# A new written order for the first two batches of a fused attention and expert-layer kernel

## The chip, the cores and the metric

The kernel runs on one core of one Trainium2 chip. The metric is the device time of one execution, in microseconds. Three runs of the kernel before took 465.88, 466.14 and 466.8 us; the median is 466.14 us. TensorE is called PE below, VectorE DVE, ScalarE ACT, GpSimd POOL and SyncE SP, as in the profile.

## What is computed

```python
def sm_attn(qq, kk, vv):
    s = scale * np.matmul(qq, kk.transpose(0, 1, 3, 2))
    a = np.exp(s - np.max(s, axis=-1, keepdims=True))
    a = a / (np.sum(a, axis=-1, keepdims=True) + 1e-09)
    return np.matmul(a, vv)
p_packed = sm_attn(p, k, v)             # 32 packed rows attend to 576 keys
out = sm_attn(q, p_packed, p_packed)    # 576 queries attend to the 32 packed rows
...
h = np.maximum(np.maximum(x @ w1, x @ w2), x @ w3)
return h @ w_out
```

There are 8 batches of 8 heads with 576 positions and a head size of 64. x is `out` with the heads of a position side by side (4608 x 512); w1, w2 and w3 are 512 x 768 and w_out is 768 x 512. All of it is float32.

## The kernel before

The kernel works batch by batch. The matrix x is never formed: `p_packed @ w` is made first (P, `project`, L439), and the second attention's weights are then multiplied with it. To keep float32 accuracy, both sides of the large products are cut into a high and a low part, and three matmuls take the place of one.

The stages of a batch, with the letters that the written order gives them:

- k, v, q, w: loads, all issued on SP's queue (L159, L165, L166, L174, L153). k of a batch comes in two transfers of 640 KB with p beside it, q in two of 576 KB, v in two of 512 KB with a small one of 64 KB each. A w chunk is 512 KB; there are 24 of them. `w02` is chunk 2 of column block 0 of w1, w2 and w3; `w60` to `w65` are w_out.
- C (`convert`): a chunk arrives as pairs of 32-bit words and is made into float32 in four steps: two on ACT (L188, L193), one on DVE (L202), one on POOL (L206). W (`weights`) prepares w_out.
- S (`scores`, L253), A (`weigh`, L266 to L271): first attention's scores, their row maximum on DVE and the exponential on ACT. The weights are then turned: in the first two batches by PE (`turn`, L296, L297) with copies out of PSUM, from the third batch on by X (`spread`): two transposes on DVE (L313) and sixteen small transfers on SP's queue (L319).
- V (`values`, L337), K (`packed`, L352): the product with v, and its turned form `pt`.
- Q (`queries`, L366), B (`attend`): second attention; nine steps on DVE, POOL and ACT for each half of the heads.
- P (`project`): `p_packed @ w` on PE, then the high part on ACT (L450) and the low part on DVE (L452).
- N (`layer_in`, L475): the main product, 36 groups of six matmuls per batch, each group into one PSUM bank. `N01` takes the next group of batch 0 and column block 1, and so on. E (`maximum`, L489, and a copy of L129 or L131): the maximum over w1, w2 and w3, which frees those banks. There are four such banks for N and for the output product together.
- H (`operands`, `halves`, L513, L134): operands of the output product. O (`layer_out`, L544): 14 groups of nine matmuls per batch. F (`finish`, L560 to L592): scaling, sums and stores.

Two tables of words, `START` and `LOOP`, set the order of everything. `run` takes the words one after another; each word takes one step of its stage's generator, so that the order of the words is the order of the instructions on each engine and on SP's queue. A last letter `v`, `g` or `a` puts the step on DVE, POOL or ACT, where the stage allows a choice:

```python
for at, word in enumerate(words.split()):
    name = word.rstrip("vga")
    chosen[0] = word[len(name):] or None
    ...
    if kind in loads:
        loads[kind](*x)
    else:
        if key not in begun:
            begun[key] = stages[kind](*x)
        next(begun[key], None)
```

`START` holds batches 0 and 1 whole, the first part of batch 2 (its first attention, its queries and some of `B20`, `B21`, `P20` to `P22`), all weights, and the k loads of batch 3. `LOOP` is run six times and holds the rest of a batch beside the beginning of the next. Words `J` and `I` with a number put that many 128-column matmuls of the identity on PE (`rouse`, L143): `J` at once, `I` ahead of the next stage that has a place for them. They compute nothing.

Buffers come from pools with a fixed number of slots: eight for k, q, v, the turned weights and the maxima ("b"), six for w chunks and w_out ("xs"). A load waits on SP's queue until the last reader of its slot is done, and all loads behind it on that queue wait too.

## Time and profile before

| What | Value |
|---|---|
| median of three runs | 466.14 us (465.88 to 466.8) |
| span of the profiled execution | 464.4 us |
| what lies around the span, against the median | 1.7 us |
| PE busy | 455.2 us (98%) |
| DVE busy | 333.5 us (72%) |
| POOL busy | 247.9 us (53%) |
| ACT busy | 159.9 us (34%) |
| granted PE clock | 1.00 |
| part set by `START` | from the beginning to the scores of batch 3, which PE starts at 141.74 us |

A profile page gives busy time by engine, the span in 40 slices of 11.6 us, and the chain of work that ended last. A busy PE also counts the identity matmuls. Matmuls of N stand in the trace as `mi` (L475), those of the output product as `mo` (L544), of P as `pw` (L439), scores of either attention as `s` (L253, L366), the product with v as `pa`, `tp` or `av` (L337).

### The profile page before, as it was taken

What the parts mean: (1) busy time and instruction counts of PE and PEld (TensorE: products, weight loads), DVE (VectorE), ACT (ScalarE), POOL (GpSimd) and SP (SyncE); (2) the same over time, 40 slices, a digit from 0 to 9 for tenths busy, and PEclk for the clock granted to TensorE, in tenths of its full rate; (3) what the DMA queues carried; (4) which work ended last, traced back from release to release, by engine and by line L of the source; (5) the groups of instructions that cost most, each with busy time, mean ns of one, the idle gap of its engine ahead of it and who ended that gap; (6) DMA issues with size and microseconds to landing.
All of it is one profiled execution on the core that took longest, in us unless ns stands there. A gap on an engine that the chain in (4) does not pass through costs nothing.

```text
span 464.4 us, 11561 instructions
## 1 busy us (share of the span) xinstructions
PE 455.2 (98%) x4724; PEld 404.9 (87%) x4724; DVE 333.5 (72%) x698; ACT 159.9 (34%) x341; POOL 247.9 (53%) x213
## 2 busy tenths in 40 slices
PE   7999998999999999999999999999999999999996
PEld 3477887899899898998899988998989988998996
DVE  1799987888887678566887479766786668845552
ACT  2787856535322126022331025121260223302130
POOL 0468875574542675526572384706764275725832
PEclk9999999999999999999999999999999999999999
DMA  8999846010316430256004450065202540020002
GB/s 313 398 382 355 321 98 230 1 58 25 95 66 195 135 119 1 80 160 233 2 27 152 87 211 2 27 199 155 94 1 94 151 116 1 28 76 1 2 6 97
DMA packets 35780, 55.66 MB, mean 120 GB/s; under 512 B 17296, under 2 KB 26512, under 8 KB 35728
## 3 DMA queue, kind: packets, MB, share of 16 engines
q1 hardware_dynamic: 35728, 54.93, 35.4%
q8 instruction: 37, 0.61, 0.5%
q14 instruction: 15, 0.12, 0.1%
HBM read 41.94 MB, written 9.44 MB: 111 GB/s over the span
## 4 chain that ended last, share of the span: by engine, by line
PE 88%; DMA 5%; SPq 3%; DVE 3%; issue 1%; ACT 1%; DVEq 0%
PE mi L475 44%; PE mo L544 29%; PE pw L439 6%; PE idle L143 2%; SPq L319 2%; PE s L366 2%; PE av L337 2%; DMA wi<-in_wi 2%; PE s L253 2%; DMA q<-in_qt 1%; DMA kt<-in_kp 1%; PE tp L296 0%; DMA xt<-x 0%; SPq L159 0%; PE pa L337 0%
## 5 line engine op out<-in xcount | busy, mean ns | idle before, releaser
L475 PE MATMUL mi<-a2h,ph 128*128 128x288 f32 x576 | 173.5, 301 | 0.8 <-DVE pl L452 0.6
L475 PE MATMUL mi<-a2l,ph 128*128 128x288 f32 x576 | 169.9, 295 | 0.0
L475 PE MATMUL mi<-a2h,pl 128*128 128x288 f32 x576 | 169.6, 295 | 0.0
L489 DVE TENSOR_TENSOR r<-mi,r 128x288 f32<-128x288 f32 x192 | 84.4, 452 | 57.8 <-PE mi L475 55.3
L475 PEld LDWEIGHTS mi<-a2h,ph 128*128 128x128 f32 x576 | 108.0, 188 | 13.4 <-issue 7.0
L475 PEld LDWEIGHTS mi<-a2l,ph 128*128 128x128 f32 x576 | 108.0, 188 | 0.2
L475 PEld LDWEIGHTS mi<-a2h,pl 128*128 128x128 f32 x576 | 108.1, 188 | 0.0
L513 POOL TENSOR_TENSOR r<-r 128x288 f32<-128x288 f32 (+1 forms) x47 | 50.4, 1083 | 81.3 <-DVE r L489 65.5
L129 ACT COPY r<-mi 128x288 f32<-128x288 f32 x73 | 29.0, 399 | 185.8 <-PE mi L475 185.7
L450 ACT ACTIVATE ph<-pw 128x384 fp32r<-128x384 f32 (+1 forms) x67 | 40.2, 631 | 46.5 <-PE pw L439 43.5
L452 DVE SCALAR_TENSOR_TENSOR pl<-pw,ph 128x384 fp32r<-128x384 f32 (+1 forms) x67 | 46.2, 713 | 9.5 <-ACT ph L450 9.2
L544 PE MATMUL mo<-ych,xl 128*128 128x288 f32 x144 | 42.5, 295 | 0.0
L544 PE MATMUL mo<-ych,xh 128*128 128x288 f32 x144 | 42.4, 294 | 0.0
L544 PE MATMUL mo<-ycl,xh 128*128 128x288 f32 x144 | 42.3, 294 | 0.0
L439 PE MATMUL pw<-w_sb,pt 64*32 64x384 f32 x768 | 36.3, 487 | 0.1
L206 POOL TENSOR_TENSOR w_sb<-w_sb,wi 128x512 int32<-128x512 int32 x18 | 23.9, 1336 | 22.0 <-DVE w_sb L202 17.4
L134 POOL TENSOR_TENSOR ybl<-r,ybh 128x576 fp32r<-128x576 f32 x15 | 21.7, 1448 | 19.7 <-DVE ybh L131 16.2
L134 POOL TENSOR_TENSOR ycl<-r,ych 128x864 fp32r<-128x864 f32 x12 | 26.6, 2218 | 5.1 <-PE mi L475 2.4
L544 PE MATMUL mo<-yah,xh 128*128 128x288 f32 x96 | 28.9, 301 | 0.0
L544 PE MATMUL mo<-yal,xh 128*128 128x288 f32 x96 | 28.4, 296 | 0.2 <-DVE yal L134 0.2
L544 PE MATMUL mo<-ybh,xh 128*128 128x288 f32 x96 | 28.3, 295 | 0.0
L544 PE MATMUL mo<-yah,xl 128*128 128x288 f32 x96 | 28.3, 295 | 0.0
(123 smaller groups left out, 808.4 us busy)
## 6 DMA issues: line engine op xcount, KB each, us to landing
kt<-in_kp SPq DMA_DIRECT2D x16, 640.0 KB, 5.4
q<-in_qt SPq DMA_DIRECT2D x16, 576.0 KB, 5.6
wi<-in_wi SPq DMA_DIRECT2D x18, 512.0 KB, 8.6
v<-in_va SPq DMA_DIRECT2D x16, 512.0 KB, 5.7
wi<-in_wo SPq DMA_DIRECT2D x6, 512.0 KB, 6.7
out_t<-r SPq DMA_DIRECT2D x8, 288.0 KB, 2.2
out_t<-t SPq DMA_DIRECT2D x8, 288.0 KB, 2.3
out_t<-s SPq DMA_DIRECT2D x8, 288.0 KB, 2.7
```

The source lines that it names most:

```text
L129: e.copy(out=out, in_=src)
L134: on(default).tensor_tensor(out=lo, in0=src, in1=hi.bitcast(F32), op=ALU.subtract)
L143: nc.tensor.matmul(out=ps[:, 0:n * P], lhsT=ident, rhs=ident.unsqueeze(1).to_broadcast([P, n, P]), start=True, stop=True,)
L206: nc.gpsimd.tensor_tensor(out=dst.bitcast(I32), in0=dst.bitcast(I32), in1=up, op=ALU.add)
L253: nc.tensor.matmul(out=s1[b][r][32 * n:32 * n + 32, hf, 0:HS], lhsT=kt[g][o, w:w + NP], rhs=kt[g][o, pr * S + hf * HS:pr * S + (hf + 1) * HS],
L439: nc.tensor.matmul(out=ps[r][NP * n:NP * n + NP, 0:NW * P], lhsT=pt_sb[b % 2][o, NP * n:NP * n + NP], rhs=w_sb[o, j, n * NW * P:(n + 1) * ...
L450: nc.scalar.activation(out=hi[:, r], in_=x, func=AF.Copy, scale=2.0 ** -WS)
L452: nc.vector.scalar_tensor_tensor(out=lo[:, r], in0=x, scalar=2.0 ** -WS, in1=hi[:, r].bitcast(F32), op0=ALU.mult, op1=ALU.subtract,)
L475: nc.tensor.matmul(out=sums[b, j, hf, x][:, 0:HS], lhsT=w[:, r, x * P:(x + 1) * P], rhs=a[:, c], start=(r == 0 and n == 0), stop=(r == R - ...
L489: nc.vector.tensor_tensor(out=h, in0=sums[b, j, hf, i][:, 0:HS], in1=h, op=ALU.max)
L513: less = lambda out, x, y: on("g").tensor_tensor(out=out, in0=x, in1=y, op=ALU.subtract)
L544: nc.tensor.matmul(out=ps[:, 0:HS], lhsT=w[:, x, m * P:(m + 1) * P], rhs=h[:, z], start=(p == 0 and i == 0), stop=(p == NQ - 1 and i == 2),)
```

## The change

Only the two tables change. No function is touched, `project` and its buffers among them. `LOOP` differs in letters that say what the stage takes anyway (`E000` is now `E000a`): on every engine the instructions from the first scores of batch 3 on stand in the same order as before. `START` is written anew. Its first and the most telling lines:

```diff
-k00 k01 I10 S0 A00 A00 J9 A00 q00 A00 w00 A01 A01 v00 J6 A01 v01 Z01 C00 C00 Z00 w02 C02 A01v V00 C00 V00 q01
+k00 k01 I10 S0 A01 w02 C02 C02 w01 C02 A00 A00 v00 v01 A01 C01 C01 C01 J18 A01 Z00 A01v C01 w00 A00 A00a q00
...
-w64 N10 C61 E110v E110 E050 H01 H01 w65 C65 C65 N11 q21 N11 N10 K2 E100v N10 H04v H04 q20 Q2 N11 w62 N10 E111
+N11 K2a q21 q20 W0a W0g Q2 W0v W0v N11 N11 w64 W0g B21 P13 B21 C64 B20 P12 N11 N11 E111v C62 C62 E050
```

In words: the first loads are k, two w chunks, v, the third w chunk and then q (before: k, one q, a w chunk, v, a w chunk, the other q). In SP's queue the chunk `w30` now stands ahead of `w12`. The second k transfer of batch 2 is the one that its scores use first. Of w_out, three chunks are loaded ahead of the sixteen transfers of `spread` (before: two), and, as before, two more stand between these and the q loads of batch 2. All N groups of batch 1 now stand ahead of the output product of batch 0 (before: the last 78 matmuls of N were mixed with it). The identity matmuls are 51 blocks of 128 columns instead of 63. DVE has six instructions more than before, POOL two and ACT four fewer.

On PE the scores of batch 2 come earlier in the program. In the rows, `mi0_2_0_2` is a group of N of batch 0, column block 2; `s1_2_0` are the scores of batch 2. Before:

```order
L475 MATMUL mi0_2_1_1_725<-a2l0_0_346,ph0_2_627 128x288
L475 MATMUL mi0_2_1_1_725<-a2h0_1_362,ph0_2_627 128x288
L475 MATMUL mi0_2_1_1_725<-a2h0_1_362,pl0_2_628 128x288
L475 MATMUL mi0_2_1_1_725<-a2l0_1_370,ph0_2_627 128x288
L253 MATMUL s1_2_0_740<-kt4_652 32x288
```

After:

```order
L476 MATMUL mi0_2_0_2_697<-a2l0_0_332,ph0_2_662 128x288
L476 MATMUL mi0_2_0_2_697<-a2h0_1_337,ph0_2_662 128x288
L476 MATMUL mi0_2_0_2_697<-a2h0_1_337,pl0_2_663 128x288
L476 MATMUL mi0_2_0_2_697<-a2l0_1_339,ph0_2_662 128x288
L254 MATMUL s1_2_0_711<-kt4_709 32x288
```

Before, 102 matmuls of N stand ahead of the scores of batch 2, now 90. The same difference of twelve stays up to batch 2's product with v (204 and 192) and its queries (246 and 234); the P stages ahead of each of these are the same.

On DVE, this stands between the maxima of batch 2's scores (`mx2`) and the transposes of `spread` (`x2`). Before:

```order
L266 TENSOR_REDUCE mx2_0_797<-s1_2_0_740 128x1
L267 TENSOR_SCALAR nm2_0_798<-mx2_0_797 128x1
L266 TENSOR_REDUCE mx2_1_804<-s1_2_1_741 128x1
L267 TENSOR_SCALAR nm2_1_805<-mx2_1_804 128x1
L400 TENSOR_REDUCE z2_1_1_0_816<-e1_1_630 128x18
L313 STREAM_TRANSPOSE x2_820<-a1_2_0_801 128x18x32
L313 STREAM_TRANSPOSE x2_820<-a1_2_1_808 128x18x32
```

After:

```order
L267 TENSOR_REDUCE mx2_0_747<-s1_2_0_711 128x1
L268 TENSOR_SCALAR nm2_0_748<-mx2_0_747 128x1
L203 TENSOR_SCALAR w_sb_72<-wi5_2_733 128x512
L267 TENSOR_REDUCE mx2_1_778<-s1_2_1_712 128x1
L268 TENSOR_SCALAR nm2_1_779<-mx2_1_778 128x1
L132 COPY r0_1_731<-mi0_3_0_0_739 128x288
L490 TENSOR_TENSOR r0_1_731<-mi0_3_0_1_754,r0_1_731 128x288
L314 STREAM_TRANSPOSE x2_814<-a1_2_0_751 128x18x32
L314 STREAM_TRANSPOSE x2_814<-a1_2_1_782 128x18x32
```

A sum over the weights moved away; a conversion step, a copy and a maximum moved in.

On SP's queue, this is the place of the sixteen transfers (`xt2`) with the w_out chunks (`wi6`) and q of batch 2 (`q5`, `q4`). Before:

```order
L153 DMA wi6_0_990<-in_wo 128x512
L319 DMA xt2_1019<-x2_820 32x5x64 x8
L319 DMA xt2_1019<-x2_820 32x4x64 x8
L153 DMA wi6_4_1105<-in_wo 128x512
L153 DMA wi6_5_1121<-in_wo 128x512
L174 DMA q5_1132<-in_qt 128x1152
L174 DMA q4_1160<-in_qt 128x1152
```

After:

```order
L154 DMA wi6_2_956<-in_wo 128x512
L320 DMA xt2_989<-x2_814 32x5x64 x8
L320 DMA xt2_989<-x2_814 32x4x64 x8
L154 DMA wi6_1_1059<-in_wo 128x512
L154 DMA wi6_3_1067<-in_wo 128x512
L175 DMA q5_1145<-in_qt 128x1152
L175 DMA q4_1147<-in_qt 128x1152
```

The queue has the same shape at this place: only which chunks stand there has changed. As before, the q loads go into slots that the product with v of the same batch leaves.

More of the change, by code (lines that the diff above doesn't have):

```diff
@@ new lines @@
+J2 V01 C00 Z01 C00 C00 C00 q01 V01 V00 V00 J1 K0 K0v J1 Q0 Q0 B000 B000 B010 B010 C02 w11 C11 C11 C11 B010v
+B001 B000g B000 B011 C11 B000 w10 C10 C10 C10 C10 P00 P00 P00 B011 w30 B000a B000 P00 B010 B010 B010v w12 C12
+C12 C12 C12 I19 P01 B000v B000 P00 w22 B010 C22 C22 B001 B000a B000v B010v B010 B010v B010g k10 P01 P01 N00
+C22 C30 C30 N00 B011v C30 B011 B001v C30 w21 k11 S1 A10 E000a A11 B011 C22 B011v B011 B011g N01 N00 w20 C20
+N01 E010v A10 A10 B001 E000 A11 C21 B001 B001v B001 A10a E010 A11 A11a v11 B001v B001 B011 B001v N01 v10 V101
@@ new lines @@
+B001v N00 B011a B011g Z10 Z11 V101 K1 E010 q10 C21 C21 C21 N00 K1a q11 Q1 C20 C20 C20 w32 C32 B10 B11 w31 C32
+C31 C31 C31 C31 C32 C32 B11 w42 E000 E001a N00 E001 E001 P10 P02 N01 N01 N01 w40 P03 C42 P02 P02 B11g N02 N02
+E011a E011 E011 w41 k21 C40 P10 P10 C41 C41 C41 C41 N02 P03 P03 C42 k20 S2 C42 C42 E020a w52 C52 C40 C40 E020
+N03 C52 A20 A20 N03 N03 P11 C52 A21 A21 E030v E030 C40 P04 N02 w60 C60 N02 X2 X2 Z21 E030 N02 C52 N03 w51 N03
+N03 E020 C51 C51 C51 H00g w50 C50 C50 C50 C50 E021a w65 P04 B10 E021 B11 E021 H02v C60 P04 N04 B11 B11v N04
@@ new lines @@
+v21 E031a B10g C51 B10 B10 B10v N04 C60 B11 B11v E040a E040 E040 P05 Z20 C65 v20 E031 E031 H01a H01g N04 E041v
+N04 w62 C62 N04 C60 P05 P05 N05 N05 C62 P11 X2 V201 B10 B10v B10 E050a N05 w61 B11 B11a B10a w63 E041 E041 N05
+N05 C61 C61 B11v H00g B10v N10 C61 V201 K2 H00g H01g E050 P11 C61 N05 E051a E100a W0v E051 E051 W0g W0v N11
+E110a N11 K2a q21 q20 W0a W0g Q2 W0v W0v N11 N11 w64 W0g B21 P13 B21 C64 B20 P12 N11 N11 E111v C62 C62 E050
+H05g P12 H03a E111 N10 E111 H01g C65 E110 N10 N10 N10 N10 E110 C65 C65 E100 P12 N12 P13 P13 N13 E101a E101
@@ new lines @@
+E101 P14 C63 C63 B21g H03v E100 P15 N12 N12 C64 C64 C63 W0v P14 P14 H04g H04a B20 E120a E120 E120 H02a C63 B21
+B21 E130v N14 N14 N14 N14 W1g E140v E140 E140 E141a H02g N14 N14 W1v W1g E141 N12 N12 N12 H04v E141 P15 C64
+E121a W2g P15 H05g N13 N13 N13 N13 W1a E121 E121 W2g W2v W2a E131a N15 W1v W1v W1v W1g E150a E130 E130 N15 N15
+W2v H05g W2a E150 W0g N15 N15 N15 E151a E151 E151 H05g H01a W2v N13 E131 E131 k31 H03v H05a H05v H03v H03v
+H03v O0 F0 O0 O0 F0 H01v W2g O0 O0 O0 F0 F0 F0 H12v E150 H13a H13g F0 O0 F0 O0 O0 H10g W2a F0 W1v F0 H12a H10a
@@ L73 @@
+H12g H13v H13v O0 O0 O0 k30 H14v W1v F0 W2g O0 O0 P20 P21 B20v F0 F0 B20 H14a B20 F0 F0 H13a F0 F0 P22 H14v
+H10v O1 O1 H11v H11v H11v H15a H15v H15v H15v O1 P21 P20 P20 H13v H11v H11v B21a H11v F1 H15a O1 O1 F1 O1 B21
+B21g H15v O1 B20a B20 P22 O1 O1 F1 F1 F1 O1 B20g P21 F1 F1 B20 F1 F1 B20g B20v F1 F1 F1 P22 O1 F1 O1 B21 B21g
+B21g P20 P20 O1 O1 F1 F1 F1
 """
 LOOP = """
[L77 to L78 removed]
@@ L84 @@
-B10g O0 O0 P12 O0 F0 F0 F0 F0 F0 B10v F0
+S1 A10 N00 E000a A11 N01 v10 E010v A10 N00 N00 N00 N00 N00 X1 A11 X1 v11 N02 N02 N02 N02 N02 E000 X1 Z10 E001a
+E001 E001 N01 E020a E020 E020 E000 H00g N01 N01 E010 E010 N01 E021a E021 H00g N01 H00g N02 P05 E011v E011 E011
+H01v H01g P03 k21 P04 V101 E021 P03 P03 P03 P03 H01g P04 N03 P04 N03 q11 H02g H01g Z11 V101 P04 P04 N04 E040a
+P05 K1 N03 N03 N03 N03 H01v N04 N04 H01g q10 E030v E030 E030 H02g E031a K1a Q1 E031 N04 E041a H02g P05 N05
+E031 E040 E040 N04 N04 B11 N05 N05 E050a B10 B10 B10v N05 N05 H03g H03g E051a E041 E041 N05 B11 P10 H03g H04v
@@ L85 @@
+H04a H03g H03a E050 E050 B10 E051 E051 H05a P10 H04v B11g P11 H03v B11 P12 P12 O0 O0 F0 O0 F0 B10 H05v H05g
+B11 H05v B11a B11 B11v H05g B10a P11 O0 H05g O0 B10 k20 B10g P10 O0 F0 P10 P10 F0 B11 B11g P11 O0 O0 F0 F0 F0
+O0 B10 O0 B11g O0 F0 F0 F0 B10g O0 O0 P12 O0 F0 F0 F0 F0 F0 B10v F0
 """
```

29 lines of the change are left out of this document (removed).

## Prediction

> **What bounds the kernel now.** I read the page first, then PE's waits, the chain of waits in order of time, the landing times of single loads, and busy time in stretches. From the page:
>
> ```profile
> span 464.4 us, 11561 instructions
> PE 455.2 (98%) x4724; PEld 404.9 (87%) x4724; DVE 333.5 (72%) x698; ACT 159.9 (34%) x341; POOL 247.9 (53%) x213
> PE   7999998999999999999999999999999999999996
> DMA  8999846010316430256004450065202540020002
> ```
>
> PE is busy almost without a break; a change of order can win only what PE spends on waits or on identity matmuls. The transfer engines are full in the first five slices (58 us) and never again. PE's waits over the whole span:
>
> ```profile
> PE s L253 <- DMA kt<-in_kp: 1.4, 1, 1.4
> PE s L366 <- DMA q<-in_qt: 1.3, 1, 1.3
> PE mi L475 <- DVE pl L452: 0.6, 1, 0.6
> PE mi L475 <- DVE r L489: 0.3, 1, 0.3
> ```
>
> The first is the wait for the first k loads. Both kernels load these first, so it stays. The second is the wait for q of batch 2 and the largest that a new order of `START` can touch. The 0.6 us lies in the last batch, outside the change. The chain in order of time (start, length, what) shows what leads to the second:
>
> ```profile
> 21.16 4.71 PE idle L143 x12
> ...
> 28.86 0.43 PE idle L143 x2
> 29.29 1.13 PE s L253 x32
> ...
> 54.04 0.74 DVE x L313
> ...
> 54.84 0.73 SPq L319
> ...
> 65.49 1.93 DMA xt<-x
> ...
> 67.47 1.51 PE av L337 x74
> ...
> 69.49 6.43 DMA q<-in_qt
> 75.92 0.14 issue
> 76.06 1.21 PE s L366 x32
> ...
> 103.66 6.37 PE mi L475 x48
> ...
> 141.74 1.13 PE s L253 x32
> ```
>
> The identity matmuls end before 29.29, where PE takes the scores of batch 1. Between 54 and 76 us the chain is not on PE at all. The transposes of `spread` end at 54.04 + 0.74 = 54.78; sixteen transfers are then issued one after another, the last lands at 65.49 + 1.93 = 67.42, the product with v ends at 68.97, and only then do the q loads get their slots. The second lands at 75.92, so that the queries start at 76.06: 21.28 us behind the end of the transposes. From 76.06 to 141.74 PE is full but for the 0.3 us. From 141.74 on the written order is the same, so the whole prediction is: when does PE reach these scores of batch 3 in the new order?
>
> **The change part by part.**
>
> *Opening.* The new first loads shift which w chunk comes when, but not how much lies ahead of the k loads of batch 1. The landing time of the second of these, and then of the one issued at 40.26:
>
> ```profile
> L159 SPq DMA_DIRECT2D kt<-in_kp x1: 424/424/424, 20.6 to 20.6; - x1
> DMA to landing us min/median/max: 8.1/8.1/8.1
> ```
>
> ```profile
> L159 SPq DMA_DIRECT2D kt<-in_kp x1: 1420/1420/1420, 40.3 to 40.3; - x1
> DMA to landing us min/median/max: 8.2/8.2/8.2
> ```
>
> The first landed at about 28.75. In both orders three other k transfers, all v and q of batch 0 and nine w chunks are ahead of it, and the engines are full, so it lands at 28.75 again. PE took it at 29.29, behind 0.43 us of identity matmuls that the new order does not have there: the scores of batch 1 start up to 0.44 us earlier. I expect 0.4 us, between nothing (if DVE's longer chain of small steps ahead of them is late) and 0.44. Dropping 12 of 63 identity blocks is otherwise free: they covered time in which PE waited for conversions and loads.
>
> *Towards batch 2.* Twelve matmuls of N fewer stand ahead of the scores, the product with v and the queries of batch 2. At 6.37/48 = 0.133 us each these are 1.6 us of work that must be done after the queries instead. For the change to break even there, the queries must start 1.6 us earlier. When they start is set by the chain above, step by step:
>
> ```profile
> 49.53 1.20 PE L253 MATMUL s<-kt 64*32 64x288 f32 x32
> ```
>
> ```profile
> 50.98 0.75 DVE L266 TENSOR_REDUCE mx<-s 128x1 f32<-128x576 f32 x1
> ```
>
> The scores of batch 2 started at 49.53. With 1.6 us less work ahead of them PE could take them at 47.9, or at 47.5 with the 0.4 us of the opening. They need `kt4`, now the second of the two k loads. In both orders six k transfers (itself among them), all v and q of two batches and fifteen w chunks make up the queue to that point, and the second one landed at 40.26 + 8.2 = 48.5. So the scores start between 47.5 (the queue runs ahead of before) and 48.6; I take 48.4, near the row, 1.1 us earlier than before.
>
> Behind the scores DVE has, between the maxima and the transposes, a conversion, a copy and a maximum more and a sum less:
>
> ```profile
> L202 DVE TENSOR_SCALAR w_sb<-wi 128x512 uint32<-128x512 uint32 x18 | 8.5, 484 | 0.2
> L131 DVE COPY r<-mi 128x288 f32<-128x288 f32 x23 | 10.4, 453 | 2.9 <-PE mi L475 2.8
> L489 DVE TENSOR_TENSOR r<-mi,r 128x288 f32<-128x288 f32 x192 | 84.4, 452 | 57.8 <-PE mi L475 55.3
> L400 DVE TENSOR_REDUCE z<-e 128x18 f32<-128x576 f32 x14 | 10.4, 743 | 0.0
> ```
>
> That is 0.48 + 0.45 + 0.45 - 0.74 = +0.65 us. Before, DVE took the first maximum 0.25 us after the scores' end (49.53 + 1.20 = 50.73 against 50.98); the new order has it directly, so +0.4 remains. The transposes end at 54.78 - 1.1 + 0.4 = 54.1, that is 0.7 us earlier; with the ends for the scores, 0.5 to 1.6 us earlier.
>
> From there nothing is shorter. The sixteen transfers, the two chunks behind them and the q loads stand as before, and q again takes its slots from the product with v. The queries start at 54.1 + 21.3 = 75.4. PE would reach the product with v about 0.7 us before its last transfer lands and the queries 1.3 us before q. The conversion that DVE now makes ahead of the scaling of this product waits for the chunk issued behind the sixteen transfers:
>
> ```profile
> L153 SPq DMA_DIRECT2D wi<-in_wo x1: 534/534/534, 66.2 to 66.2; - x1
> DMA to landing us min/median/max: 4.2/4.2/4.2
> ```
>
> That is 65.5 + 4.2 = 69.7, with 0.7 us for the ACT step, so that four maxima and the scaling stand behind it in DVE's queue and PE meets a full set of banks for about 1 us. It lies inside the time that PE waits for q anyway and is counted at nothing; if q came 1 us sooner, it would be the wait.
>
> So at the queries the new order is 1.6 - 0.7 = 0.9 us behind, between 0 and 1.1.
>
> *After the queries.* 198 instead of 186 matmuls of N remain, the twelve counted above. The old wait of 0.3 us in the N groups at 90 us belongs to an order that is gone: I take -0.25, between -0.3 and a wait as large as in the rival below.
>
> Sum: 0.9 - 0.25 = 0.65 us on a span of 464.4, so 465.05. The median is 466.14 and thus 1.74 us above the span; the time is 466.8 us.
>
> **The rivals.** About 0.2% (0.9 us) is what a measurement here can tell from no change.
>
> *Faster: the queue behind the transfers is emptier.* Three w_out chunks instead of two are already loaded ahead of the sixteen. If q then lands as quickly as the first chunk did (4.2 us instead of 6.43), the queries start 2.2 us sooner and the time is 466.8 - 2.2 = 464.6. For it: all that remains between the product and q is those transfers. Against it: two 512 KB chunks still stand directly ahead of q, as before, and DVE's late conversion takes back up to 1 us.
>
> *Slower: DVE becomes the bound behind the queries.* Busy time in two stretches (total, then PE, PEld, DVE, ACT, POOL):
>
> ```profile
> 76.00:104.00 28.00, 27.68 (x268) 24.58 (x269) 24.20 (x46) 14.76 (x27) 18.55 (x17) 1.00 0.10 35
> 104.00:141.74 37.74, 37.74 (x324) 36.11 (x329) 32.63 (x60) 13.30 (x25) 20.65 (x15) 1.00 0.18 59
> ```
>
> DVE is at 86% in both. Before, the last 78 matmuls of N ran mixed with the output product, which needs DVE less. Now all 198 run in one piece of about 29 us (26.3 us, and four P stages): 33 groups of six pass through DVE where 18 did before the output product began, and every three groups need two maxima there. Four banks let PE run ahead by little more than three groups (2.4 us). Once DVE is behind by more, PE waits at each group. Where POOL is at work beside it DVE's own steps stretch:
>
> ```profile
> 119.61 2.43 DVE L513 TENSOR_TENSOR r<-r 128x288 f32<-128x288 f32 x2
> L513 DVE TENSOR_TENSOR r<-r 128x288 f32<-128x288 f32 x14 | 7.0, 501 | 0.0
> ```
>
> Two steps took 2.43 us there instead of 1.0. One such pair more, beside the 0.25 us that I gave back, makes 1.4 + 0.25 = 1.65 us, and the time 468.5. It decides as soon as DVE's share between the queries and the output product passes about 95%. [...]
>
> *Slower: PE's clock falls in a gap.* With 12 identity blocks fewer PE may stand still for longer before the second P stage.
>
> ```profile
> 1.36 3.83 PE L143 MATMUL s<-ident 128*128 128x512 f32 x6 [1.36 <-POOL ident masks.py:199]
> 21.09 4.78 PE L143 MATMUL idle<-ident 128*128 128x512 f32 x12
> ```
>
> The first ten blocks took 0.38 us each, the 21 later ones 0.23. If a gap brings the early pace back for as long (3.83 us), it costs 3.83 x (1 - 0.23/0.38) = 1.5 us: 468.3. Against it: the queries after 1.3 us of waiting took 1.21 us, near the 1.13 us of other scores, and 12 x 0.23 = 2.8 us is the most that all gaps together grow. [...]
>
> **How the numbers follow.** Forecast (within 0.2%): 0.42. Queue emptier: 0.22. DVE bound: 0.30. Clock: 0.06. So faster 0.22, same 0.42, slower 0.36. The range takes in the faster rival at 464.6 and the slower ones at 468.5, with 0.1 and 0.2 us for scatter: 464.5 to 468.7.
>
> **What would show it.** Right: the second k load of batch 2 lands near 48.5 and the scores start right behind it; the transposes end near 54.1; the queries start near 75.4, still waiting for q; PE reaches the scores of batch 3 near 142.4. Wrong: queries before 74.4, or that point before 141 (the faster rival); many short waits of N for DVE's maxima between 76 and 105 us (the slower one); N matmuls at more than 0.133 us after a gap near 24 us (the clock).

## The result and the profile after

| | Before | After |
|---|---|---|
| median | 466.41 us (465.88 to 466.8, four runs) | 471.97 us (471.29 to 472.21, four runs) |
| ratio | | 1.0118, 95% interval 1.0104 to 1.0133 |
| span of the profiled execution | 464.4 us | 470.0 us |
| around the span | 1.74 us | 1.74 us |

The new order is 1.2% slower. The forecast was 466.8 us, the range 464.5 to 468.7; the result lies 3.3 us above the range. The scores of batch 1 came as predicted, and what followed did not.

The page after. Line numbers are those of before plus one:

```profile
span 470.0 us, 11548 instructions
PE 457.3 (97%) x4716; PEld 404.8 (86%) x4716; DVE 336.9 (72%) x704; ACT 159.9 (34%) x337; POOL 244.6 (52%) x211
PE   8889998999999999999999999999999999999996
DMA  8999945001415340166004360064202530020002
```

By the averages almost nothing has happened. Of the 5.6 us, PE shows 2.1 as busy time, although it has eight matmuls fewer. The second and third slices of PE are at 8 instead of 9, where the identity matmuls went; the transfer engines are at 9 instead of 8 in the fifth, which now ends at 59 us.

PE's waits after (who waits for whom: total, times, longest):

```profile
PE mi L476 <- DVE r L490: 1.2, 1, 1.2
PE mi L476 <- DVE pl L453: 1.2, 2, 0.6
PE av L338 <- DMA xt<-x: 0.8, 1, 0.8
PE pw L440 <- ACT a L272: 0.7, 1, 0.7
```

The wait for q (1.3 us before) is gone. In its place stand three others between 53 and 75 us: 1.2 and 0.6 us for DVE and 0.7 us for ACT (of the second row one of its two 0.6 us; the other is that of the last batch, as before). The 0.8 us for a small transfer lies in the seventh batch, at 380 us. The chain of waits in order of time, at the places of which the prediction gave a time:

```profile
28.92 1.27 PE s L254 x32
...
53.71 1.34 DVE x L314 x2
...
73.69 1.02 PE mi L476 x6
74.83 2.38 PE mi L476 x18
77.21 1.24 PE s L367 x32
...
109.44 16.76 PE mo L545 x126
126.20 2.10 PE pw L440 x48
128.29 17.22 PE mo L545 x126
145.51 1.13 PE s L254 x32
```

| Point | Before | Predicted | After |
|---|---|---|---|
| scores of batch 1 | 29.29 | 28.9 | 28.92 |
| second k load of batch 2 landed | 48.50 | 48.5 | 46.51 |
| scores of batch 2 | 49.53 | 48.4 | 48.61 |
| transposes end | 54.78 | 54.1 | 55.05 |
| queries of batch 2 | 76.06 | 75.4 | 77.21 |
| scores of batch 3 | 141.74 | 142.4 | 145.51 |
| from there to the end | 322.66 | 322.66 | 324.49 |

So the distance from the forecast's span (465.05 us) is made of three parts: 77.21 - 75.4 = 1.81 up to the queries; 68.30 us instead of 67.0 from the queries to the scores of batch 3, 1.30; and 1.83 behind them. 465.05 + 1.81 + 1.30 + 1.83 = 469.99.

**Up to the queries.** The second k load of batch 2 landed 5.9 us after its issue at 40.58, not 8.2:

```profile
L160 SPq DMA_DIRECT2D kt<-in_kp x1: 383/383/383, 40.6 to 40.6; - x1
DMA to landing us min/median/max: 5.9/5.9/5.9
```

So it was there 2.1 us before the scores of batch 2, and these came at 48.61 because PE came to them then. It had lost its time further ahead: from the scores to the queries of batch 1 it took 10.01 us (28.92 to 38.93), before 9.68 (29.29 to 38.97), with six matmuls of N fewer, 0.8 us. That is 1.1 us in all; the chain is on DVE there, from 30.18 to 37.45.

DVE's timeline behind the scores of batch 2 (start, length, what):

```profile
49.93 0.76 DVE L267 TENSOR_REDUCE mx<-s 128x1 f32<-128x576 f32 x1 [0.46 <-PE s L254]
...
50.80 1.12 DVE L203 TENSOR_SCALAR w_sb<-wi 128x512 uint32<-128x512 uint32 x1
51.85 0.75 DVE L267 TENSOR_REDUCE mx<-s 128x1 f32<-128x576 f32 x1
...
52.70 0.45 DVE L132 COPY r<-mi 128x288 f32<-128x288 f32 x1
53.25 0.46 DVE L490 TENSOR_TENSOR r<-mi,r 128x288 f32<-128x288 f32 x1
53.62 1.43 DVE L314 STREAM_TRANSPOSE x<-a 128x576 f32<-128x576 f32 x2
```

The steps are those of the forecast, but the conversion took 1.12 us, not the mean of 0.48, while POOL was at its own conversion steps (four of 1.3 us from 47.2 on). A busy POOL alone does not explain it: in the kernel before one conversion beside a POOL step took 1.21 us (at 38.4) and another 0.43 (at 50.6). The transposes end at 55.05.

The sixteen transfers behind them became slower too. The slowest of them landed after 5.8 us instead of 3.9, and the last issue started 11.0 us behind the first instead of 10.7. The transfer engines were fuller (the last two columns are their share and GB/s). After:

```profile
49.90:76.00 26.10, 23.41 (x266) 20.08 (x266) 24.72 (x51) 16.41 (x31) 15.88 (x14) 1.00 0.70 220
56.00:60.00 4.00, 3.86 (x30) 3.63 (x28) 3.86 (x8) 3.54 (x8) 3.19 (x3) 1.00 0.95 283
```

Before:

```profile
50.90:76.00 25.10, 23.75 (x273) 21.09 (x272) 22.08 (x50) 15.41 (x32) 17.60 (x14) 1.00 0.68 219
56.00:60.00 4.00, 4.00 (x39) 3.73 (x29) 3.52 (x8) 2.22 (x5) 4.00 (x4) 1.00 0.37 77
```

Between 56 and 60 us they are at 0.95 instead of 0.37: a third w_out chunk stands ahead of the sixteen, and v of batch 2 is issued at 50.7 instead of 42.3 us, behind w chunks for whose slots SP waits. But PE did not wait for these transfers: the last was issued at 66.12 and landed 1.94 us later, at 68.06, and PE came to the product with v at 68.44, straight from matmuls of N.

What the chain shows from 50.8 to 73.6 us is DVE's queue. Some of its steps:

```profile
59.48 0.94 DVE pl L453
...
66.94 1.83 DVE e L410
68.79 1.44 DVE et L413 x2
...
71.71 0.75 DVE a2l L135
...
73.18 0.38 DVE r L490
...
```

`e`, `et` and `a2l` are steps of batch 1's second attention, and the last row is the maximum for which PE waits 1.2 us. q has landed at 76.29 (70.48 + 5.8), and PE comes to the queries 0.9 us later. Over the whole stretch DVE (the third busy time) is at 95% instead of 88%. From the scores to the queries PE took 77.21 - 48.61 = 28.6 us; before 26.5, with the same work between them.

**Behind the scores of batch 3** the batches 3 to 6 take 54.08, 54.10, 54.07 and 54.21 us instead of 54.03. The seventh batch, after:

```profile
361.97 1.27 PE s L254 x32
...
376.56 4.10 DMA xt<-x
...
380.79 1.41 PE av L338 x74
```

Before:

```profile
357.85 1.13 PE s L253 x32
...
375.59 1.39 PE av L337 x80
```

The product with v starts 18.82 us behind the scores instead of 17.74, because the last small transfer took 4.10 us to land (PE waits 0.8 us for it); in the batches 3 to 6 of both kernels the last ones took 1.9 to 2.8, and in batch 7 of before 2.9 to 3.7, just in time. This is 1.08 of the 1.83 us.

### The profile page after: what moved, and what is told of

Read it like the earlier page. It is cut to its first block, busy times and chain, and to the rows that moved or that the text cites. A ratio compares the mean times of both kernels' runs of the same rounds, so it can differ in the third digit from the quotient of the medians.

```text
span 470.0 us, 11548 instructions
## 1 busy us (share of the span) xinstructions
PE 457.3 (97%) x4716; PEld 404.8 (86%) x4716; DVE 336.9 (72%) x704; ACT 159.9 (34%) x337; POOL 244.6 (52%) x211
## 4 chain that ended last, share of the span: by engine, by line
PE 80%; DVE 10%; DMA 4%; SPq 2%; issue 1%; ACT 1%; POOL 0%; DVEq 0%; POOLq 0%; ACTq 0%
PE mi L476 40%; PE mo L545 29%; PE pw L440 5%; DMA wi<-in_wi 3%; PE s L254 2%; SPq L320 2%; PE s L367 2%; DVE r L490 2%; PE av L338 2%; DVE mx L267 1%; PE s L144 1%; DMA xt<-x 1%; DVE pl L453 1%; DVE et L413 1%; DVE e L410 1%
## 5 line engine op out<-in xcount | busy, mean ns | idle before, releaser
L514 POOL TENSOR_TENSOR r<-r 128x288 f32<-128x288 f32 (+1 forms) x49 | 52.8, 1088 | 81.3 <-DVE r L490 65.1
L451 ACT ACTIVATE ph<-pw 128x384 fp32r<-128x384 f32 (+1 forms) x67 | 40.1, 632 | 51.7 <-PE pw L440 48.7
L545 PE MATMUL mo<-yal,xh 128*128 128x288 f32 x96 | 28.4, 296 | 0.2 <-DVE yal L135 0.2
L545 PE MATMUL mo<-ybh,xl 128*128 128x288 f32 x96 | 28.3, 295 | 0.0
```

Source lines behind the costliest of these rows:

```text
L451: nc.scalar.activation(out=hi[:, r], in_=x, func=AF.Copy, scale=2.0 ** -WS)
L514: less = lambda out, x, y: on("g").tensor_tensor(out=out, in0=x, in1=y, op=ALU.subtract)
L545: nc.tensor.matmul(out=ps[:, 0:HS], lhsT=w[:, x, m * P:(m + 1) * P], rhs=h[:, z], start=(p == 0 and i == 0), stop=(p == NQ - 1 and i == 2),)
```

## The experiments

All times in us; starts by PE's timeline (up to 0.1 ahead of the chain's rows) in the one execution of each run that was profiled. The ratio is to the kernel before and takes in all executions. They lie up to 4.1 us apart (i2: 470.07 to 474.21), and the profiled one of e8 is 1.4 us faster than its next, so that a microsecond between two starts of this table can be one of the execution and not of the edit. "Rest" is from the scores of batch 3 to the end.

| Run | Scores 2 | Queries 2 | Scores 3 | Rest | Ratio (95%) |
|---|---|---|---|---|---|
| before | 49.5 | 76.1 | 141.7 | 322.7 | |
| after | 48.6 | 77.1 | 145.4 | 324.5 | 1.0118 (1.0104 to 1.0133) |
| e1_loop | 49.8 | 76.0 | 141.6 | 322.7 | 1.0003 (0.999 to 1.0016) |
| e2_frontQ1 | 50.0 | 78.5 | 146.8 | 323.3 | 1.0115 (1.0092 to 1.0138) |
| e3_backQ2 | 48.5 | 77.1 | 146.6 | 325.9 | 1.0156 (1.0133 to 1.0179) |
| e4_c52 | 48.6 | 77.5 | 145.8 | 324.4 | 1.0125 (1.0103 to 1.0147) |
| e5_order | 53.4 | 86.6 | 166.9 | 323.0 | 1.0547 (1.0531 to 1.0563) |
| e6_letters | 52.4 | 82.9 | 156.5 | 322.8 | 1.0329 (1.0309 to 1.0348) |
| e7_shift | 49.6 | 75.9 | 149.3 | 322.7 | 1.017 (1.0153 to 1.0187) |
| e8_max | 48.8 | 77.5 | 145.8 | 323.9 | 1.0144 (1.0121 to 1.0167) |
| f1_phase | 50.1 | 79.1 | 147.4 | 323.2 | 1.0105 (1.0081 to 1.0128) |
| f2_v | 48.7 | 78.8 | 148.1 | 324.9 | 1.0148 (1.0122 to 1.0175) |
| f4_all | 50.1 | 82.2 | 150.5 | 323.2 | 1.0176 (1.0153 to 1.0199) |
| g1_z | 49.6 | 76.1 | 141.7 | 322.7 | 0.9992 (0.9975 to 1.0009) |
| h1_noez | 49.0 | 77.7 | 145.9 | 324.1 | 1.0109 (1.0093 to 1.0125) |
| h2_B1v | 50.0 | 78.8 | 144.4 | 323.8 | 1.0055 (1.0036 to 1.0075) |
| h3_B1 | 48.8 | 82.2 | 150.8 | 324.3 | 1.02 (1.0179 to 1.022) |
| h4_m8 | 51.2 | 77.8 | 143.5 | 322.8 | 1.0008 (0.9995 to 1.0022) |
| i1_w65 | 48.4 | 77.5 | 145.7 | 324.2 | 1.0137 (1.011 to 1.0165) |
| i2_both | 48.8 | 77.2 | 145.5 | 324.1 | 1.0101 (1.0061 to 1.0142) |

### Which part of the tables

**`LOOP` alone** (`START` of before).

> The LOOP table of the change alone, with START of before. Theory START (all of the loss starts in START; LOOP's rows are the same): the time of before, 466.4 us within 0.3, the scores of batch 3 at 141.7 and about 54.03 us for each later batch. Rival LOOP (its letters cost something, since the change also lost some 1.5 us behind the scores of batch 3): 467.5 to 468 us, with one or more batches over 54.1 us.

466.52 us, and the rest unchanged at 322.7. The letters of `LOOP` cost nothing; all of the loss comes from `START`, that behind it too.

**The opening of before up to the first queries of batch 1**, the new order from there.

```diff
-k00 k01 I10 S0 A01 w02 C02 C02 w01 C02 A00 A00 v00 v01 A01 C01 C01 C01 J18 A01 Z00 ...
+k00 k01 I10 S0 A00 A00 J9 A00 q00 A00 w00 A01 A01 v00 J6 A01 v01 Z01 C00 C00 Z00 w02 ...
```

> Before's order up to the queries of batch 1, then what is left of START in the change's order. Between the scores and the queries of batch 1 the change took 10.0 us with 36 matmuls of N, before 9.7 us with 42: 1.1 us of its loss. Theory late binding (what sets the time lies behind the scores of batch 2: maxima, transposes, sixteen transfers, q): PE gets there earlier but waits for the second k load of batch 2, and little comes through: 471.5 us, within 0.5 of the whole change. Rival opening (PE's lost work there is lost for good): 470.9 us, 1.1 us faster than the whole change.

As slow as the change, so the opening is not the cause. The equal total hides two differences, though: the scores of batch 3 come 1.4 us later than in the change (PE waits 1.0 us for a maximum ahead of the scores of batch 2), and the rest is 1.2 us shorter, of which the next section tells.

**The order of before from the queries of batch 2 on.**

```diff
-E110a N11 K2a q21 q20 W0a W0g Q2 W0v W0v N11 N11 w64 ...
+E110a N11 K2a q21 q20 W0a W0g Q2 w64 N10 E110 E050 H01 C65 N11 N11 ...
```

> The change's order up to the queries of batch 2, then what is left of START in before's order (the last N groups of batch 1 mixed with the output product again). Up to the queries as in the change (77.1 us). Theory DVE-bound stretch (the change lost 1.0 us between these queries and the scores of batch 3 because all N groups stand in one piece): 67.3 us instead of 68.3 us from the queries to these scores, which come at 144.4, and 471.0 us. Rival backlog (the loss there is DVE's backlog from ahead of the queries, whatever follows): 68.2 us or more for the stretch and 472.0 us.

Slower still, at 473.56 us: 69.5 us from the queries to the scores of batch 3, although the last N matmuls are mixed with the output product again. So the theory falls, and the stretch is as the rival said (68.2 us or more). PE waits there for DVE's low parts and for a maximum:

```profile
PE mi L475 <- DVE pl L452: 1.2, 2, 0.6
PE mi L475 <- DVE r L489: 0.3, 1, 0.3
```

The kernel before, with the same order in this stretch, has the 0.3 us alone. In the change and in eight of the runs that keep its order there the stretch takes 68.3 us, with queries anywhere between 77.1 and 82.2 us (69.3 in f2, 68.6 in h3); before it was 65.7 with twelve matmuls of N fewer. That it is nearly constant speaks for the order of the stretch, e3 for what DVE has left over from ahead of the queries. No run separates the two, and that N in one piece is the reason isn't shown.

**The new order with the letters of before, and the reverse.**

```diff
-C52 A21 A21 E030v E030 ... B11 B11v N04 v21 E031a B10g C51 B10 B10 B10v
+C52 A21 A21 E030 E030 ... B11 B11 N04 v21 E031 B10 C51 B10 B10 B10
```

(for one line of e5; e6 is the same exchange in the tables of before)

> The change's order of steps, with each step on the engine that it had before (the letters of START taken back step by step, the order kept). Theory engine choice: the change also put steps of batch 1's second attention (the two products e with z, the low parts a2l) on DVE, and they stand in the 27 us from the scores to the queries of batch 2 in which DVE has no idle time; without them the queries of batch 2 start at 75.5 to 76.2 instead of 77.1 and the time is 470 us or less. Rival order: what counts is where steps stand; DVE is as full, the queries stay at 77 us and the time at 472 us.

> Before's order of steps, with each step on the engine that the change gives it. Theory engine choice: most of the loss comes back, 469 to 470 us, and DVE is full between the scores and the queries of batch 2. Rival order: the choice of engines costs nothing by itself, 466.4 us within 0.5.

+5.5% and +3.3%: each is far worse than both kernels, and neither theory nor rival came near. Part of e5's loss is PE's clock: it was granted at 0.50 in two stretches of 6.8 us, from 27.0 and from 91.8 us. Order and engine letters fit only together, and what one of them "costs" has no answer of its own.

### The loss behind the scores of batch 3

**Before, made later** by identity matmuls at the end of `START`.

```diff
-... F1 F1 P21 F1 F1 B21 B21 B20v F1
+... F1 F1 P21 F1 F1 B21 B21 B20v F1 J9 J9 J9 J9
```

> Before, with 36 blocks of the identity (twelve matmuls, 3.5 to 4.2 us) on PE between the last matmul of START and the scores of batch 3, so that LOOP starts as late as in the change. Theory time of day (in each batch one of the sixteen transfers stalls by 1 to 1.8 us, and it depends on the start of LOOP which one it is; the change lost 1.2 us where it was the last of batch 7): a batch of 54.5 us or more comes, and the time is 471.0 to 471.6 us. Rival (LOOP's loss has another cause in the change): all batches 54.03 us, and 466.4 + 3.9 = 470.3 us.

The batches start 7.6 us later, twice as much as was meant, and their periods are as before (rest 322.7). No batch lost time to a later start. The run added 24 matmuls on PE, and so led to the next theory: something that goes by the number of PE's instructions. The queues on the page of the change have this row (packets, MB, share):

```profile
q8 instruction: 37, 0.61, 0.6%
```

And in its window from 377.5 to 378.0 us the queues moved:

```profile
q1 hardware_dynamic: 95, 0.02, 24.8%
q8 instruction: 1, 0.02, 19.1%
```

Queue 8 moves 37 packets of 16 KB (0.61 MB in all) in the span. Were they PE's alone, that would be one for each 9432/37 = 255 of its 4716 matmuls and as many weight loads; no view names the engine of this queue, so this is an estimate, and whether the packet moves with the number of PE's matmuls is for f1 and h4 below to show. One packet falls into this half microsecond and takes 0.191 x 16 x 0.5 = 1.5 us of one engine's time (in e8, where little was lost, 12.1% and 1.0 us), while the last small transfer (issued at 376.56) is under way. That transfer is the one for which PE waits 0.8 us.

**The change with eight `J1`**, in the trace sixteen matmuls more (4732), so that the packet comes earlier.

```diff
-C12 C12 C12 I19 P01 B000v B000 P00 w22
+C12 C12 C12 I19 P01 J1 J1 J1 J1 J1 J1 J1 J1 B000v B000 P00 w22
```

> The change with eight more matmuls of the identity (128 columns, 0.8 us in all) on PE, where it waits 0.9 us for a conversion at 24.8 to 25.7 us; nothing else moves. Theory fetch: the queue for instructions moves 37 packets of 16 KB, one for about 255 of PE's 9432 instructions, and the one at 377.5 us stands beside the last of the sixteen transfers of batch 7, which then lands after 4.1 us instead of 1.9, so that PE waits 1.1 us; with eight matmuls (sixteen instructions) more ahead, the packet comes 1 us earlier in the batch, as before the change, and the batches take 54.03 to 54.1 us each again with no wait for that transfer: 470.9 us. Rival (another cause in LOOP): the loss in batch 7 stays, 472.0 us.

Its seventh batch, in the chain:

```profile
363.75 1.13 PE s L254 x32
...
381.49 1.39 PE av L338 x80
```

17.74 us, as before: the loss is gone, and nothing but sixteen matmuls at 27 us was added. The total doesn't fall, since these matmuls themselves made the scores of batch 1 1.5 us later.

**Before with sixteen matmuls fewer** (4708), so that the packet comes later.

```diff
-v00 J6 A01 ... C12 C12 J21 P01
+v00 A01 ... C12 C12 P01
```

> Before without eight matmuls of the identity (two groups, ahead of the second turning of batch 0's weights and ahead of the first N groups), so that PE has as many instructions as in the change. Theory fetch: the packet of instructions that stands at 372 us in before comes eight matmuls (1.1 us) later in its batch, as in the change, beside one of the last two of the sixteen transfers of batch 7, and that batch loses 0.8 to 1.2 us; the scores of batch 3 stay near 141.7 if the groups only covered waits: 467.3 to 467.6 us. Rival: LOOP is untouched, 466.4 us, or up to 1.5 us more if PE's clock falls in the new gaps, with the loss ahead of 30 us.

Eight fewer were meant, which would have made 4716 as in the change, and a loss in batch 7 was expected; the trace has sixteen fewer. The packet moved by 3.0 us, from 14.5 to 17.5 us behind the scores of batch 7, past all of the sixteen, and cost nothing. So the packet comes later with fewer matmuls, as the count asks, and at 17.5 it meets nothing.

This run also shows what the identity matmuls are for. PE waits 3.4 us for conversions between 18 and 31 us, and its granted clock (the third column from the end) falls to 0.50; in the kernel before it is 1.00 there:

```profile
23.20:30.00 6.80, 5.31 (x22) 2.77 (x23) 5.84 (x16) 5.62 (x14) 4.82 (x6) 0.50 1.04 405
```

The scores of batch 1 come 1.7 us later in this execution (468.05 us; the median of twelve is 466.85), as the rival had it.

All runs together (packet and product with v in us behind the chain's row for the scores of batch 7; landing of the last small transfer where it was read):

| Runs | PE matmuls | Packet | Landing | Product with v |
|---|---|---|---|---|
| before, e1, e6, g1, h2 | 4724 | 14.5 to 15.1 | 2.9 (before) | 17.7 |
| e2 | 4724 | 14.5 | | 18.1 |
| f1, f4 | 4732 | 14.3 | | 17.7 |
| e7 | 4748 | 11.8 | | 17.7 |
| h4 | 4708 | 17.5 | | 17.7 |
| after | 4716 | 16.0 | 4.1 | 18.8 |
| e4, f2, h1, h3, i1 | 4716 | 15.8 to 16.2 | 3.8 to 3.9 | 18.5 to 18.6 |
| i2, e3 | 4716 | 15.7 to 15.8 | 3.3 to 3.6 | 18.2 to 18.3 |
| e8 | 4716 | 15.7 | 3.1 | 17.7 |
| e5 | 4716 | 16.7 | 1.9 | 17.7 |

The last transfer is issued at 14.6 us. A packet that starts about then or sooner meets earlier transfers as well, which have more time (e2 alone lost 0.4 us); one at 17.5 meets none; with one at 15.7 to 16.2 the last one landed after 3.1 to 4.1 us. It is not certain at every such place: e8 lost only 0.2 us, with queries 26.8 us behind its scores instead of 26.6, and e5, at 16.7, nothing. Why isn't shown; no view tells the sixteen engines apart. The time of day is no rival: f4 and h3 start these batches 0.3 us apart (150.5 and 150.8), and only h3, with 4716 matmuls, loses.

The packet is not the only thing that can make a small transfer late. In e3 the fifth batch took 55.84 us: its sixteen transfers were issued 1.3 us later than in the change (the last at 16.3 us behind the scores), and the last one, beside a packet at 17.3, landed after 3.1 us. Why they were issued late stays open.

### The stretch between the scores and the queries of batch 2

**The conversion moved from between the maxima to behind the transposes.**

```diff
-N03 C52 A20 A20 N03 N03 P11 C52 A21 A21 ... N02 X2 X2 Z21 E030
+N03 C52 A20 A20 N03 N03 P11 A21 A21 ... N02 X2 X2 C52 Z21 E030
```

> The change with one step moved: the conversion on DVE that stands between the two maxima of batch 2's scores now stands behind the two transposes of spread. Theory chain (scores, maxima, transposes, transfers, q decide when the queries of batch 2 start): the transposes end 1.0 us earlier (54.0 instead of 55.05), PE's 0.8 us wait for the last transfer and most of the 0.7 us wait for the exponential go, the queries start at 76.2 instead of 77.1, and the time is 471.1 us. Rival full queue (DVE has no idle time from 48 to 75 us, so the step only comes back in front of the scaling of the product with v, and PE's 1.2 us wait there grows by it): queries at 77.0 to 77.2 and 472.0 us.

The transposes did end at 54.0 us, but SP then waited 1.2 us more between the transfers (for w_out and for DVE), so that their issue took 12.9 us, and PE's wait for the low part of P grew to 1.5 us:

```profile
PE mi L476 <- DVE pl L453: 2.1, 2, 1.5
PE mi L476 <- DVE r L490: 1.2, 1, 1.2
```

(the first row holds the 0.6 us of the last batch too). Queries at 77.5: no gain.

**The maximum that frees the last bank moved ahead of the two low parts** of batch 1's weights on DVE.

```diff
-N05 C61 C61 B11v H00g B10v N10 C61 V201 K2 H00g H01g E050 P11
+N05 C61 C61 E050 B11v H00g B10v N10 C61 V201 K2 H00g H01g P11
```

> The change with one step moved: the maximum for which PE waits 1.2 us at 73.69 now stands ahead of the two low parts, the late conversion and the scaling on DVE. Theory (this wait is what delays the queries of batch 2, since q has landed at 76.3 us and PE comes at 77.1): queries at 76.3 and 471.2 us. Rival of the prediction (the wait lies inside the time that PE would wait for q anyway): queries at 77.0 or later, waiting for q, and 472.0 us.

```profile
PE mi L476 <- DVE r L490: 0.8, 1, 0.8
```

The wait shrank from 1.2 to 0.8 us and came two microseconds later. q landed at 77.0, and the queries started at 77.5, still behind that wait and not waiting for q. No gain: the rival's time, though not its wait.

**v of batch 2 ahead of the first w_out chunk.**

```diff
-N02 w60 C60 N02 X2 X2 ... N04 v21 E031a ... C65 v20 E031
+N02 v21 v20 w60 C60 N02 X2 X2 ... N04 E031a ... C65 E031
```

(shown against the order of after, as all in this section)

> The change with the two v loads of batch 2 moved on SP's queue from behind three w chunks that wait for slots to ahead of them. Theory transfer backlog (the transfer engines are full until 59 us, 3 us longer than before, because SP stood 6 us on slots with v behind it, so that the first of the sixteen transfers land after 5.8 us and the last at 68.4): engines free by 57, the first transfers land after 4 us, the last at 67.4 to 67.7, PE's wait of 0.8 us there is gone, the queries of batch 2 start at 76.3 and the time is 471.2 us. Rival full DVE (PE is held by DVE's steps in the same stretch anyway): queries at 77.0 and 472.0 us.

```profile
PE mi L476 <- ACT r L130: 1.2, 1, 1.2
```

Worse: the w chunks behind v land later, ACT waits 1.7 us at 49.9 for one of them, PE then waits for ACT, and its wait for the low part of P grows to 1.4 us.

**f1, f2, e8 and e4's step at a later place (behind the next low part of P), together.**

> The change with four edits at once: v ahead on SP's queue, the conversion between the maxima moved behind the low part of P04, the maximum ahead of the two low parts, eight identity matmuls. Theory parallel paths (from the scores to the queries of batch 2 three paths, SP's queue with the transfers, DVE's queue and PE's own order, end within 1 us of each other, so that one edit alone gains nothing): together the queries start at 75.2 to 75.9, the scores of batch 3 at 144, and the time is 468.5 to 469.5 us. Rival (DVE's load as such): queries at 76.5 or later and 471 us.

1.0176, the queries at 82.2 us: the repairs get into each other's way.

**Before with one sum moved off the path** to the transposes, and two steps with it.

```diff
-A20 A20 A21 A21 w50 C50 w51 B11 B11 B10 X2 X2 C50
+A20 A20 A21 A21 w50 C50 w51 X2 X2 B11 B11 B10 C50
```

> Before with one sum over weights (0.74 us on DVE) and two small steps moved from ahead of the two transposes of spread to behind them. Theory chain (in before the chain from the scores of batch 2 over the transfers and q sets the start of its queries): transposes end at 54.0 instead of 54.8, the last transfer lands near 66.7, the product with v ends 0.4 us earlier and the queries start at 75.6: 465.9 us, 0.1% faster, at the edge of what can be told. Rival (parallel paths, or a full transfer queue): 466.4 us and queries at 76.0.

No difference (queries at 76.1). The transposes ended at 53.7 instead of 54.8, but PE came to the product with v only at 68.0, with nothing but its own work since a low part of P at 58.9. So in the kernel before, too, a second path ends within 0.6 us of the transfers (the product at 67.47), and ending the transposes earlier wins nothing.

**Less work for DVE.** h1 leaves out the scaling of batch 1's weights on DVE:

```diff
-        on("v").tensor_tensor(out=e3, in0=e3, ...)
+        if b != 1:
+            on("v").tensor_tensor(out=e3, in0=e3, ...)
```

> The change without the two products of batch 1's second attention with the reciprocal sums (0.76 and 1.82 us on DVE at 62.7 and 66.9 us); batch 1 is left without this scaling, nothing takes its place. Theory DVE's queue (DVE has no idle time from 49.9 to 75 us, and what PE waits for at 60.5 and 73.7 us is the end of that queue): PE's wait of 1.2 us at 73.7 goes, the queries of batch 2 wait for q and start at 76.3, and the time is 471.0 to 471.2 us. Rival (each engine's order, not DVE's load): within 0.3 us of the change, 472.0 us.

The maximum's wait fell to 0.8 us, and PE waited for the small transfers (0.7 us) and for q (0.3 us) instead; queries at 77.7. The chain is now that of the prediction, but later: the last transfer lands at 68.97, the product ends at 70.52, and q takes 6.49 us from 71.03 on. That DVE alone is the bound falls.

**The engines of the two halves of batch 1 exchanged** (ten letters of `B10` and `B11`): those of the change in before (h2), those of before in the change (h3).

```diff
-B11 v20 B11 E040v E040 B10 ... B10g B10 B11 H00
+B11 v20 B11a E040v E040 B10 ... B10a B10v B11v H00
```

(the middle of h2)

> Before, with only the second attention of batch 1 (B10, B11) on the engines that the change chose for it: the products with the reciprocal sums, the low parts and two small sums move from POOL and ACT to DVE, some 4.3 us of DVE work between 52 and 73 us. Theory DVE's queue: the scaling of batch 2's product with v comes 2 to 3 us later than at 69.0, the queries at 77.3 to 78 instead of 76.1, and the time is 468 us. Rival: DVE takes it in its free time (0.9 us ahead of the scaling, and PE has 1.3 us of waiting for q to give): 466.5 us.

> The change with only the second attention of batch 1 back on the engines that it had before. Theory DVE's queue: 2 to 4 us of DVE work less ahead of the scaling of batch 2's product with v, PE's wait at 73.7 us goes, queries at 76.3 (q lands there), 471.0 to 471.3 us. Rival (POOL and ACT are then what PE waits for): 472.0 us or more.

In before, the letters of the change cost 2.8 us at the queries. PE's largest new wait is the 1.5 us in this row (the rest of it is the last batch's, as before):

```profile
PE mi L475 <- DVE pl L452: 2.0, 2, 1.5
```

In the change the old letters make it worse, by 5 us at the queries: PE waits 3.2 us for maxima, and behind the longest of these waits (2.6 us) its granted clock is 0.50 from 79.4 to 82.8 us, ahead of the queries. So DVE's load there is a cost, and in the new order this distribution is still the better one.

**A w_out chunk taken away ahead of the transfers**: `w65` and its first ACT step behind q and the queries.

```diff
-C50 C50 E021a w65 P04 B10 ... K2a q21 q20 W0a W0g Q2 ...
+C50 C50 E021a P04 B10 ... K2a q21 q20 w65 W0a W0g Q2 ...
```

> The change with one w_out chunk fewer ahead of the sixteen transfers (two, as before): its load now stands behind q of batch 2, its first ACT step behind the queries. Theory two paths (transfers and DVE's queue each hold PE in the stretch, within a microsecond of each other): the transfer engines are free 1.4 us sooner (57.5 instead of 59), the last of the sixteen lands at 67.6 to 67.9 instead of 68.4 and PE's 0.8 us wait there goes, but the wait of 1.2 us for DVE at 73.7 stays or grows, the queries start at 76.6 to 77.1 and the time is 471.6 to 472.0 us. Rival transfers alone: the queries start 0.8 us earlier, 471.2 us or less.

The transfer engines between 56 and 58 us, with the chunk away (the last two columns; in the change 1.03 and 365):

```profile
56.00:58.00 2.00, 2.00 (x18) 2.00 (x17) 1.90 (x5) 1.54 (x4) 1.44 (x2) 1.00 0.57 148
```

And PE's waits for maxima in the whole run:

```profile
PE mi L476 <- DVE r L490: 1.9, 2, 1.2
```

The engines are emptier, and the last of the sixteen lands at 67.9 instead of 68.1. PE had not waited for them in the change (the 0.8 us that the expectations of e4, f2 and i1 place here are those of batch 7), so nothing was to be won there; a second wait for a maximum came in (1.2 us at 64.7), and the queries start at 77.5. The transfers alone are not the bound either.

**Both, h1 and i1.**

> The same, and the two products of batch 1's second attention with the reciprocal sums left out as in h1 (batch 1 stays without this scaling). Theory two paths: only with both edits do the queries of batch 2 come earlier, at 75.6 to 76.2, 1 us or more ahead of the change, and the time is 470.2 to 471.0 us. Rival (a third path, such as q itself, ends as late): queries at 76.9 or later and 471.6 us or more.

```profile
PE pw L441 <- ACT a L272: 0.8, 1, 0.8
PE mi L477 <- DVE r L491: 0.7, 1, 0.7
PE s L367 <- DMA q<-in_qt: 0.5, 1, 0.5
```

Queries at 77.2, and PE waits for q again. The chain leaves DVE at 60.8 us, behind the low part of P for which PE waits 0.6 us; from there it is PE's own work up to the product with v at 68.34, and then q, which takes 6.56 us from 70.52 on. So with the maximum's wait shortened the way over the product and q ends at 77.1, and the way over DVE in the change ended at 77.2. Counted from the scores, PE comes to the product 19.5 us later in i2, in the kernel before 17.5; two waits, 0.8 us for the exponential at 54 us and the 0.6 us, are 1.4 of these 2.0. No run took all of the waits away at once.

## Why the prediction was wrong

**The opening: right.** The scores of batch 1 came 0.37 us earlier (0.4 predicted), because the identity blocks ahead of them were gone.

**"So the scores start between 47.5 ... and 48.6; I take 48.4": the number is right by luck.** Two steps failed and nearly cancel. The k load did not land at 48.5, like the row of before, but at 46.51, and PE was not there at 47.5: it lost 1.1 us between the scores and the queries of batch 1 (38.93 against 38.97 before, with six matmuls of N fewer), where the chain is on DVE. The prediction had named DVE's chain of small steps as a risk ahead of the scores of batch 1, and had no term for it behind them.

**"The transposes end at ... 54.1": 0.95 us too early.** 0.2 is from the scores, 0.64 from one conversion of 1.12 us that I priced at the group's mean of 0.48, 0.1 from a wait. I had looked for longer steps beside POOL only in the rival of DVE, in a pair of L513 with two inputs each (2.43 us: 0.52 for 128x288 and 1.87 for 128x576, where others of before took 0.45 and 0.75); this step has one input, and took longer beside POOL too. What makes it longer isn't shown: of two such steps beside POOL in the kernel before one took 1.21 us and the other 0.43.

**"From there nothing is shorter ... 54.1 + 21.3": this is the step that failed, by another 0.86 us.** It took the 21.28 us over whole, as if the chain of before (transfers, product, q) were the only one, and it let PE reach the product ahead of the last transfer and the queries ahead of q. The runs show another path in its place. PE waited 0.7 us for the exponential and 0.6 for a low part of P, and came to the product at 68.44, behind the last transfer (68.06); then it waited 1.21 us for a maximum at the end of DVE's queue, and 24 matmuls of N ended at 77.21, when q had been there since 76.29. The prediction had seen a wait of about 1 us here and counted it at nothing, as lying inside the wait for q; with PE last there was nothing left to hide it. Its reason was another as well: the late conversion took 0.42 us, and ahead of it stood two low parts of batch 1 (`a2l`, 1.2 us). Taking away this path alone wins nothing, since the way over the product and q then ends at 77.1 to 77.5 (i2, h1). i1, h1, e8 and e4 each shortened one part and gained nothing, i2 two (28.4 us from scores to queries; 28.4 to 33.4 in all runs of the new order there, 26.5 before). What would bring back the 26.5 stays open.

**"After the queries ... -0.25": failed by 1.30 us.** The direction of the slow rival was right, and its mechanism appears in small. From 102.4 to 107.0 us PE made 30 matmuls of N, of the long piece, in 4.60 us, where 0.133 us each make 4.0; DVE is without a pause there, and the chain has its maximum directly ahead of PE's next group:

```profile
102.40:107.00 4.60, 4.43 (x30) 3.73 (x29) 4.09 (x7) 1.59 (x5) 3.31 (x4) 1.00 0.34 115
```

```profile
103.61 0.38 DVE r L490
...
104.04 2.65 PE mi L476 x18
```

That is 0.6 us, in waits too short for a row of their own. The second set of 126 output matmuls takes 17.22 us instead of 16.88; the rest is spread. Mixing N with the output product again doesn't bring the loss back (e3), and why DVE is late in this stretch stays open.

**"From 141.74 on the written order is the same, so the whole prediction is: when does PE reach these scores": the largest single error, 1.83 us.** The written order is the same, but it isn't all that PE's instructions meet. 1.08 us is the instruction packet beside the last small transfer of batch 7, shown by f1 (loss gone with sixteen more matmuls) and by the table over the runs; the prediction put what lies behind batch 3 at nothing, without a reason beyond the order. Of the other 0.75, 0.35 lies in the four periods of batches 3 to 6 (54.08 to 54.21 us instead of 54.03; the output product takes 16.92 instead of 16.87), 0.1 in the rest of batch 7 and 0.30 in the tail; these weren't tested. Some 0.04 us a batch is in every run that has the new order between the queries of batches 1 and 2 (in e2 and e3 too) and in none that has the old one.

**The rivals.** Faster by an emptier queue: the two q loads landed 5.0 and 5.8 us after their issue instead of 5.6 and 6.4, so the shorter transfer existed, but q was no longer what PE waited for. The clock: 0.998 was granted over the span, with no fall near 24 us, and the queries took 1.24 us against 1.21. That this rival was real is shown by h4, where dropping sixteen identity matmuls of before did bring the clock to 0.50 for 6.8 us: no wait there is longer than 1.7 us, though there are three in six microseconds, and in h3 the clock was 0.50 for 3.4 us right behind one of 2.6 us. No run shows how long a gap must be for that. The pace of the first ten blocks, from which the 1.5 us were worked out, was no sign of it: the clock granted there (1.36 to 5.2 us in the kernel before) is 1.00. The chances of 0.30 for DVE and 0.06 for the clock were my estimates. `LOOP`: nothing, as said (e1).

## What to carry to other kernels

A chain that ends with one wait says nothing about the path that comes second: before "t + 21.3" is carried into a new order, add up the slack of each engine in that stretch, as a change that takes 1 us of cover from three of them can be lost on any. Before a number counts as confirmed, check its two halves: here a load came 2 us sooner and PE 1 us later than thought, and the start between them looked right. Price a step beside a busy POOL by the rows beside POOL, short and long (here 0.43 to 1.21 us), not by the mean of its group (0.48). And where the number of PE's instructions changes, look at the places where PE waits for a single small transfer, however far behind the edit: here sixteen matmuls more or fewer moved an instruction packet by 1.7 and 3.0 us, 350 us behind the edit.
